# Strassen's seven block products for gate and value of two sequences, with TensorE in the order of the program text

## Chip, cores, metric

One core of one Trainium2 chip. The metric is the device time of one execution in microseconds (us), as the median of several runs. All timed runs quoted here were in the fast state; single looks (one run, state unknown) are marked as such.

## The reference

Attention with normalised q and k over 8 sequences of 448 tokens and 12 heads of 64, followed by a gated feed-forward layer. All in float32 on the chip; the weights arrive in 8-byte form and are converted on the chip.

```python
batch, n_heads, seq, head_dim = (8, 12, 448, 64)       # attention
n_tokens, d_model, d_ff = (3584, 768, 1536)            # feed-forward

scores = scale * np.matmul(rmsnorm(q, g_q), rmsnorm(k, g_k).transpose(0, 1, 3, 2))
attn = softmax(scores)                                 # cut: max, exp, sum
x = np.matmul(attn, v)                                 # (B,H,S,D) -> (B*S, H*D)
xn = x / rms(x) * rms_g
g = xn @ w_gate
return (g * (1 / (1 + np.exp(-g))) * (xn @ w_val)) @ w_out
```

## The kernel before

A program text that mixes two streams: attention of sequence b, pair of heads by pair, and feed-forward items of sequence b-1, put into four slots of each pair by `fill()`. The scheduler of the framework then orders each engine by priority and simulated readiness. The parts that matter:

```python
ps_s, ps_m, ps_f = pool("c_ps_s", 4, space=PSUM), pool("c_ps_m", 2, space=PSUM), pool("c_ps_f", 2, space=PSUM)
...
def turn(g, i):                     # transpose q or k of a pair
    ps = ps_m.tile([128, NT, P], F32, name="tr", tag="m")
    ...                             # four transposes; i == 0: ScalarE copies, i == 1: VectorE copies
def values(g):
    av = st["av", g] = ps_m.tile([128, 512], F32, name="av", tag="m")
    ...                             # e @ v, then den = sums of e (four terms in the first sequence, else one)
def divide(g):
    nc.vector.reciprocal(rd, den[:, 0:S])
    nc.vector.tensor_tensor(x, av[:, 0:S], rd, ALU.mult)
    ...                             # x*x on ScalarE, ss += on GpSimd
def project(b, fc, w):              # one of 12 column blocks of gate or value
    ps = st[w, b, fc] = ps_f.tile([128, 512], F32, name="ff", tag="ff")[:, 0:S]
    for c in range(NDC):            # 6 matmuls
        nc.tensor.matmul(ps, lhsT=wt[:, c, :], rhs=st["xT", b][:, c, :], start=(c == 0), stop=(c == NDC - 1))
...
for g in range(NG):                 # 48 pairs
    score(g, (0, 1)); norm_pair(g + 2); fill()
    turn(g + 1, 0); fill()
    if g: finish(g - 1)             # values, divide, fill
    turn(g + 1, 1); score(g, (2, 3)); fill()
```

`convert` turns a weight block to float32: a DMA, then ScalarE, GpSimd, VectorE twice, ScalarE, GpSimd. In the kernel before a third of the blocks is converted beside sequence 0's attention, the rest beside its feed-forward.

## Time and profile before

| | kernel before |
|---|---|
| time | 1848.26 us median (1848.02 to 1853.11, 4 runs) |
| TensorE busy | 1778.2 us, 96% |
| to the first gate matmul | 138 us, sequence 0 alone |
| 138 to 300 us | units beside conversion, 21 us of TensorE idle |
| 300 us to the end | TensorE never idle until its last matmul, 432.9 us for two sequences, 216.4 for one |

How to read it: "busy" on TensorE hides gaps shorter than a matmul's modelled end, so I go by spacings, start to start. Most lines are in the prediction. The first gate matmuls of sequences 2, 4 and 6 start at 602.45, 1035.33 and 1468.20 us. Windows, columns: length; TensorE, weight load, VectorE, ScalarE and GpSimd, each as busy us and records; clock, DMA share, GB/s.

### The profile page before, as it was taken

To read this page: it belongs to the slowest core of one execution; us is meant where nothing else is said; L and a number is where in the kernel's file an instruction comes from. 1 tells how busy PE (TensorE), PEld (TensorE's weight loads), DVE (VectorE), ACT (ScalarE), POOL (GpSimd) and SP (SyncE) were. 2 spreads that over 40 slices of the span, in tenths; PEclk is the share of its full clock that TensorE was granted. 3 is DMA by queue.
4 is the path that set the end of the run, shared out by engine and by line. 5 is a ranking of instruction groups with operands and counts; after the bars stand their busy time and mean duration, and the time that the engine had idled before them with its cause. 6 is when DMAs were issued, how large, how long until landed. Compare 5 with 4: busy or idle time off the path is not lost. (4 is left out here: it accounts for less than half of the span.)

```text
span 1848.4 us, 15816 instructions
## 1 busy us (share of the span) xinstructions
PE 1778.2 (96%) x5960; PEld 880.4 (48%) x5960; DVE 510.6 (28%) x546; ACT 441.8 (24%) x725; POOL 638.1 (35%) x527
## 2 busy tenths in 40 slices
PE   5878989999999999999999999999999999999998
PEld 2333434544455444554455544554445544455554
DVE  3646664122212222123212222222221222111100
ACT  5643442122121313112221122212222122210000
POOL 6765774324232424322432243323234133210000
PEclk9888999999999999999999999999999999999999
DMA  5625653122220323113321232212231132202200
GB/s 157 219 76 156 194 190 99 32 82 80 87 55 27 90 83 93 46 53 88 87 65 38 66 91 83 68 41 84 84 90 41 41 87 67 69 18 74 88 9 28
DMA packets 154475, 149.00 MB, mean 81 GB/s; under 512 B 95509, under 2 KB 124693, under 8 KB 154389
## 3 DMA queue, kind: packets, MB, share of 16 engines
q1 hardware_dynamic: 153280, 147.88, 27.6%
q8 instruction: 50, 0.82, 0.2%
q14 instruction: 37, 0.29, 0.1%
q10 hardware_dynamic: 1108, 0.00, 0.0%
HBM read 127.41 MB, written 20.45 MB: 80 GB/s over the span
## 5 line engine op out<-in xcount | busy, mean ns | idle before, releaser
L578 PE MATMUL ff<-xT,wg 128*128 128x448 f32 x1152 | 457.0, 547 | 7.3 <-DVE ga L587 7.2
L578 PE MATMUL ff<-xT,wv 128*128 128x448 f32 x1152 | 456.6, 546 | 3.4 <-DVE hT L593 3.4
L603 PE MATMUL ff<-wo,hT 128*128 128x384 f32 x1344 | 444.6, 488 | 0.0
L603 PEld LDWEIGHTS ff<-wo,hT 128*128 128x128 f32 x1344 | 251.6, 190 | 182.2 <-issue 14.9
L578 PEld LDWEIGHTS ff<-xT,wg 128*128 128x128 f32 x1152 | 215.7, 191 | 231.6 <-issue 212.0
L578 PEld LDWEIGHTS ff<-xT,wv 128*128 128x128 f32 x1152 | 214.3, 191 | 229.6 <-issue 215.3
L511 POOL TENSOR_TENSOR es<-es,e 112x448 f32<-112x448 f32 x168 | 187.0, 1145 | 289.3 <-ACT e L501 289.3
L501 ACT ACTIVATE e<-sc,rs 112x448 f32<-112x448 f32 x384 | 214.2, 636 | 160.8 <-PE sc L497 160.7
L497 PE MATMUL sc<-qkT 64*112 64x448 f32 x768 | 185.4, 590 | 21.8 <-DVE qkT L487 15.2
L546 POOL TENSOR_TENSOR ss<-ss,s 128x448 f32<-128x448 f32 x40 | 46.6, 1164 | 427.4 <-ACT s L545 427.4
L535 DVE RECIPROCAL rd<-den 128x448 f32<-128x448 f32 x48 | 141.9, 2956 | 180.6 <-PE den L526 180.6
L519 PE MATMUL av<-e,vt 112*64 112x448 f32 x768 | 159.1, 557 | 0.0
L466 POOL TENSOR_TENSOR rs<-ms,mhalf 112x16 f32<-112x16 f32 x48 | 140.4, 2926 | 4.0
L585 ACT ACTIVATE th<-ff 128x448 f32<-128x448 f32 x96 | 52.0, 541 | 342.5 <-PE ff L578 342.4
L587 DVE SCALAR_TENSOR_TENSOR ga<-th,ff 128x448 f32<-128x448 f32 x96 | 59.2, 617 | 252.8 <-ACT th L585 252.8
L593 DVE SCALAR_TENSOR_TENSOR hT<-ga,ff 128x448 f32<-128x448 f32 x96 | 59.3, 618 | 236.5 <-PE ff L578 232.6
L463 DVE TENSOR_REDUCE ms<-sq 112x16 f32<-112x1024 f32 x48 | 58.5, 1219 | 216.8 <-ACT sq L460 201.2
L497 PEld LDWEIGHTS sc<-qkT 64*112 64x112 f32 x768 | 66.7, 180 | 104.4 <-issue 58.0
L507 POOL TENSOR_TENSOR es<-e 112x448 f32<-112x448 f32 x84 | 94.1, 1140 | 50.7 <-ACT e L501 50.7
L545 ACT ACTIVATE s<-xT 128x448 f32<-128x448 f32 x40 | 23.1, 577 | 327.7 <-DVE xT L540 327.7
L519 PEld LDWEIGHTS av<-e,vt 112*64 112x64 f32 x768 | 52.0, 140 | 97.7 <-issue 97.4
L468 POOL TENSOR_TENSOR qn<-qk,rs 112x512 f32<-112x512 f32 x48 | 51.4, 1070 | 80.8 <-PE tr L482 79.8
(46 smaller groups left out, 709.9 us busy)
## 6 DMA issues: line engine op xcount, KB each, us to landing
wg<-kept_g SPq DMA_DIRECT2D x84, 384.0 KB, 3.0
wv<-kept_v SPq DMA_DIRECT2D x84, 384.0 KB, 3.0
qk<-in_q_dram SPq DMA_DIRECT2D x96, 112.0 KB, 3.3
qk<-in_k_dram SPq DMA_DIRECT2D x96, 112.0 KB, 3.2
vt<-in_v_dram SPq DMA_DIRECT2D x48, 224.0 KB, 2.6
raw<-in_moe_w_gate_dram SPq DMA_DIRECT2D x12, 768.0 KB, 5.9
raw<-in_moe_w_val_dram SPq DMA_DIRECT2D x12, 768.0 KB, 4.8
raw<-in_moe_w_out_dram SPq DMA_DIRECT2D x12, 768.0 KB, 4.5
```

The source lines that it names most:

```text
L463: nc.vector.tensor_reduce(out=ms, in_=sq.rearrange("p (n d) -> p n d", d=D), axis=AX_X, op=ALU.add)
L466: nc.gpsimd.tensor_tensor(rs, ms, mhalf[0:P, :], ALU.pow)
L497: nc.tensor.matmul(ps, lhsT=qkT[r, 1, c * P:(c + 1) * P], rhs=qkT[r, 0, :], start=True, stop=True)
L501: nc.scalar.activation(e, ps, ACT.Exp, scale=rs[:, n:n + 1])
L507: nc.gpsimd.tensor_tensor(es, st["e", g, 0, j], st["e", g, 1, j], ALU.add)
L511: nc.gpsimd.tensor_tensor(es, es, st["e", g, c, j], ALU.add)
L519: nc.tensor.matmul(av[j * D:(j + 1) * D, 0:S], lhsT=vt[:, j, c, :], rhs=st["e", g, c, j], start=(c == 0), stop=(c == NT - 1))
L535: nc.vector.reciprocal(rd, den[:, 0:S])
L578: nc.tensor.matmul(ps, lhsT=wt[:, c, :], rhs=st["xT", b][:, c, :], start=(c == 0), stop=(c == NDC - 1))
L587: nc.vector.scalar_tensor_tensor(ga, th, 1.0, g, ALU.add, ALU.mult)
L593: nc.vector.scalar_tensor_tensor(hT[:, fc, c0:c0 + S], st.pop(("ga", b, fc)), 0.5, st.pop(("v", b, fc)), ALU.mult, ALU.mult)
L603: nc.tensor.matmul(ps, lhsT=hT[:, fc, i * 128:(i + 1) * 128], rhs=wo[:, fc, n * HALF:(n + 1) * HALF], start=(fc == 0), stop=(fc == NFC - 1))
```

## The change

Intent: with two sequences stacked, gate (and value) is a 2x2 block product: rows are two sequences, the inner dimension is cut in half, and column block fp is paired with fp+6. Strassen's form (Winograd's variant) needs seven products of half the size instead of eight, so 1/8 of the matmuls of gate and value go. To keep the order in which products follow each other, TensorE is taken from the scheduler and runs in the order of the text. What it takes: feed-forward can start only after two sequences, the weights are stored as seven combined blocks and loaded from DRAM for each two sequences, and the eight PSUM banks are split 4, 1 and 3 instead of 4, 2 and 2. Conversion now goes by half blocks, with two buffers for raw words instead of three.

```diff
-    ps_s, ps_m, ps_f = pool("c_ps_s", 4, ...), pool("c_ps_m", 2, ...), pool("c_ps_f", 2, ...)
+    ps_s, ps_m, ps_f = pool("c_ps_s", 4, ...), pool("c_ps_m", 1, ...), pool("c_ps_f", 3, ...)
+    ORDER = ("B11", "T2", "B21", "T3", "T4", "T1", "B22")
@@ turn
-        ps = ps_m.tile([128, NT, P], F32, name="tr", tag="m")
+        ps = (ps_f if i == 1 and g <= ALONE else ps_m).tile(...)        # ALONE: sequences 0 and 1
@@ in place of project, gate, val
+    def product(k, fp, w, left, right, bank, onto=False):              # 3 matmuls; onto: adds to the bank
+        def p1(): product(.., "A11", "B11", fresh("a")); nc.scalar.copy(add["p1"], bank["a"])
+        def p6(): product(.., "S2", "T2", fresh("b")); plus("u2", bank["b"], "p1")
+        def p2(): product(.., "A12", "B21", bank["a"], onto=True); hand(0, 0, bank["a"])
+        def p7(): product(.., "S3", "T3", fresh("c")); plus("u3", bank["c"], "u2")
+        def p4(): product(.., "A22", "T4", fresh("d")); plus("c21", bank["d"], "u3"); hand(1, 0, add["c21"])
+        def p5(): product(.., "S1", "T1", fresh("e")); plus("c22", bank["e"], "u3")
+        def p3(): product(.., "S4", "B22", bank["e"], onto=True); plus("c12", bank["e"], "u2"); hand(0, 1, ..); hand(1, 1, ..)
+        return [p1, p6, p2, p7, p4, p5, p3]
@@ ffn_items: 84 products spread over 24 slots of the next sequence, 14 output items over those of the one after
+    AHEAD, LEFT = 14, 3
@@ before the main loop
+    ctx.enter_context(tc.manual_schedule(engines={mybir.EngineType.PE}))
@@ weights: conversion of units 0 and 1 in sequence 1; the rest, and the output weight, in sequence 2
```

(cut: loading, left factors, the rest of `ffn_items`)

## The prediction

> **What bounds the kernel now.** I read the page first (shares, forty slices), then the busy time by windows, then the time line of single stretches. The page says that TensorE is the bound, and the slices say where it is not.
>
> ```profile
> PE 1778.2 (96%) x5960; PEld 880.4 (48%) x5960; DVE 510.6 (28%) x546; ACT 441.8 (24%) x725; POOL 638.1 (35%) x527
> PE   5878989999999999999999999999999999999998
> PEclk9888999999999999999999999999999999999999
> ...
> L578 PE MATMUL ff<-xT,wg 128*128 128x448 f32 x1152 | 457.0, 547 | 7.3 <-DVE ga L587 7.2
> L578 PE MATMUL ff<-xT,wv 128*128 128x448 f32 x1152 | 456.6, 546 | 3.4 <-DVE hT L593 3.4
> ```
>
> The second view is the busy time by windows:
>
> ```profile
> 138.00:300.00 162.00, 141.27 (x432) 64.70 (x432) 101.70 (x88) 67.36 (x98) 111.03 (x82) 0.92 0.55 171
> 300.00:1627.00 1327.00, 1327.00 (x4511) 659.81 (x4511) 316.85 (x354) 289.21 (x498) 429.39 (x366) 1.00 0.24 68
> ```
>
> So three stages. To 138 us (the first gate matmul) one sequence's attention runs alone. From 138 to 300 gate and value of sequence 0 run while weights are still converted: 21 us of TensorE idle, clock 0.92. From 300 on TensorE never rests: 1327/6 = 221.2 us a sequence, at full clock. The change takes TensorE work away, and it pays only where TensorE stays this full. Whether it does is the question.
>
> The third view is the time line of TensorE and VectorE:
>
> ```profile
> 1675.86 4.67 PE L578 MATMUL ff<-xT,wv 128*128 128x448 f32 x12
> 1680.37 4.67 PE L578 MATMUL ff<-xT,wg 128*128 128x448 f32 x12
> ```
>
> Start to start is 4.51 us for 12 records. A float32 matmul is two records (1152 records, 576 matmuls), so one is 0.752 us and one product of three matmuls 2.26 us. In the same way an output item of 24 records is 7.79 us, a score call 1.69, av 3.06, den from summed e 0.85, four transposes 0.45: a pair is 2x1.69+2x0.45+3.06+0.85 = 8.2, a sequence with its norm 50.8. The steady stage then is 24x4.51+7x7.79+50.8 = 213.5 us by spacings against 221.2 measured: 7.7 us a sequence go at switches between kinds.
>
> **What the Trainium skill says.** "TensorE: Matmul & The Clock Gate", Part 1, says that the array falls to half clock after an idle window of about 3.4 us. The trace agrees: the first line below needs 6.47 us for what takes 4.7, so such a gap costs 1.8 us more.
>
> ```profile
> 202.19 6.47 PE L578 MATMUL ff<-xT,wg 128*128 128x448 f32 x12 [3.75 <-DVE ga L587]
> ```
>
> The same page, Part 2, says that matmuls stay in program order and only weight loads are pulled ahead; and, under "Architectural detail", that ScalarE and VectorE are strict first in, first out. So a matmul whose bank is not free holds all behind it; the line above is such a wait. "PSUM — Partial Sum Buffer", on the has_written bits, says that a matmul without the first flag adds to what is there; the change uses this to save two additions per unit. It is not exercised like that before, so no trace shows it yet. "Advanced Engine Details and Errata", "VectorE Performance Modes", says that VectorE's second SBUF port is shared with GpSimd and they block each other. The conversion's shift agrees: 0.55 us alone, 2.19 beside a GpSimd addition of 1.85.
>
> **The change, part by part.** Two sequences are one 2x2 block product; "unit" is my word for seven products of gate or value (12 units for two sequences).
>
> Removed: 48 items of 4.51 us become 84 products of 2.26, so 216.5 -> 189.4 us per two sequences, **27.1 us saved, 108 us in all**. Output work is the same (14 items for two sequences, 109 us).
>
> Added on VectorE: five additions and four hand-overs of 0.62 us a unit, 5.6 us beside 15.8 us of matmuls. Not a bound by itself. But three things now wait in TensorE's fixed order.
> (a) Products p5 and p3 stand next to each other, and p3 adds onto p5's bank after VectorE has read it (c22). The loss is 0.16 drain + 0.1 start + 0.62 + 0.05 (VectorE's ga ended at 165.33, the matmul started at 165.38) = 0.95 us a unit, 48 units: 46 us. No slot falls between the two: the fill rule gives 3, 4, 3, 4 products, so it breaks after p2 and after p3. p2 onto p1's bank has p6 between, no wait.
> (b) The pool of transposes and av has one bank instead of two. In program order the second transpose of the next pair follows av and den, and needs av's bank. The chain behind den, and the one that the row norm needs, stand here:
>
> ```profile
> 1008.28 2.96 DVE L535 RECIPROCAL rd<-den 128x448 f32<-128x448 f32 x1 [11.53 <-PE den L526]
> 1011.27 0.62 DVE L540 TENSOR_TENSOR xT<-av,rd 128x448 f32<-128x448 f32 x1
> 1011.99 0.58 ACT L545 ACTIVATE s<-xT 128x448 f32<-128x448 f32 x1 [7.13 <-DVE xT L540]
> 1012.64 1.13 POOL L546 TENSOR_TENSOR ss<-ss,s 128x448 f32<-128x448 f32 x1 [14.98 <-ACT s L545]
> ```
>
> The bank comes free 3.7 us after den's end, ss 5.6 us after. In the sequences that fill with products every slot has 7 or 9 us of work and covers this. In those that fill with output items, 11 items go to 24 slots: by the rule to slots 2,4,6,8,10,13,15,17,19,21,23. The slot after av and den is each fourth one, so it is filled at 4 and 8 and empty at 12, 16, 20 and 24. Three empty ones cost 3.7+1.8 (cold clock) = 5.5 each, the last one waits for ss, 5.6+1.8 = 7.4; three empty slots between the first transpose and av cost some 1.0 each, two between the score calls 1.0 each. **29 us in each of three such sequences, 87 us.**
> (c) Sequences 0 and 1 run without filler. A pair there has four den terms, 3.0 instead of 0.85: 10.4 us of work, plus 2.1 waiting for av's bank behind four exponentials, plus 2.3 because the copy of the second transpose queues behind the reciprocal, plus 2 for the clock: 17 us (18.0 in the kernel before, 63.75 to 81.73, with two conversions a pair).
>
> Stages, in us:
> 1. To the first product: 16 start, 6 for the first pair, 11x17, then scores, av, den, ss chain, norm and score calls of the next, 26: **235**.
> 2. Sequence 2 with 84 products and conversions: 189.4+50.8+7.7+12x0.95 = 259. Here fall 64 half blocks of conversion. VectorE: 64x1.3 (94.5 us for 36 full blocks) = 83, 40 subtractions estimated at 0.5 = 20, units 67, attention 33, norm 4: 207 of 259, 80%, against 63% in the window 138 to 300, where 24 full blocks cost 34 us of idle and slow clock. I choose 41 us of loss: **300**.
> 3. Sequences 3, 5, 7 with output items: 109+50.8+4+29 = 193 each, **579**.
> 4. Sequences 4, 6 with products: 259 each, **518**.
> 5. The tail: 189.4+11.4+109+7 (the end after the last matmul, as now) = **317**.
> Sum **1949**. Against 1848: -108 saved, +13 for den terms, and the rest is waiting.
>
> **Rivals.** (R1) The saving survives: the waits of (a) and (b) are covered because other engines run ahead, and conversions hide. The 2-unit lead of the conversions and the 14 blocks of weights asked ahead speak for it; that the order is the text's speaks against. Stages 210+265+3x165+2x248+306 = 1772 us. (R2) Conversion becomes the bound of stage 2: two raw buffers instead of three, each held from the DMA (4.5 to 5.9 us to landing for a full block) through six operations. In the window 138 to 300 a full block took 6.75 us with three buffers. If a half block takes 6 us with two, 64 take 384 us and the total is some 2030. Against it: half sizes and more lead. (R3) Weights from DRAM hold TensorE: a block of 192 KB per 2.26 us is 87 GB/s, and 231 GB/s have been moved in the trace, while 384 KB landed in 3.0 us. With 14 blocks ahead I expect nothing of it. (R4) Only one of (a) and (b) is real: about 1865 to 1905.
>
> **Range and chances.** I lean from the sum a little towards R1, since waits estimated one by one overlap: 1935 us, 8 in 10 between 1835 and 2030. The lower end is half of (a) and (b) with a stage 2 without loss; the upper is R2. Faster by over 2% (under 1811) needs R1 nearly whole: 0.12. Within 2%: 0.20. Slower: 0.68.
>
> **What would show it.** In the changed profile: 2016 gate and value matmul records for 1152x2 = 2304 times 7/8 (right by counting); the first product near 235 us; idle of TensorE before p3 by VectorE's c22, 48 times near 0.8 us; idle before the second transpose by VectorE's x, some 3.5 us, three times in each of sequences 3, 5 and 7, with a clock under 1.0 there; slices of 7 to 8 tenths in these stretches and 9 in sequences 4 and 6. I am wrong if TensorE stays full from 300 us on, if the bank waits are absent, or if the first stages take under 470 us (R1) or over 600 us (R2) in sum.

## More of the kernel before

```profile
602.40:1035.30 432.90, 432.90 (x1474) 215.48 (x1472) 104.55 (x117) 95.31 (x165) 143.27 (x121) 1.00 0.25 70
1035.30:1468.20 432.90, 432.90 (x1475) 215.50 (x1473) 104.56 (x117) 95.42 (x165) 143.24 (x121) 1.00 0.25 70
```

Two sequences are compared with 432.9 us below.

## The result

The changed kernel took **2000.6 us** (1998.36 to 2005.86, 4 runs), the kernel before 1848.26. The ratio is 1.082, 95% interval 1.079 to 1.085. Here and below a ratio is the mean of one kernel's fast runs over the mean of the other's of the same rounds, so it is not quite the ratio of the medians. The time lies inside the range, towards its upper end; slower was the direction with chance 0.68.

The page of the changed kernel (busy time, slices of 50 us, granted clock):

```profile
PE 1749.4 (87%) x5744; PEld 854.5 (43%) x5744; DVE 713.7 (36%) x966; ACT 482.1 (24%) x897; POOL 615.7 (31%) x559
...
PE   5767687778689988999999988999999998999998
...
PEclk8788888899889988999999988999999998999999
...
L624 PE MATMUL ff<-x,wt 128*128 128x448 f32 x2016 | 807.5, 554 | 107.2 <-DVE c L638 98.3
```

2016 gate and value records, 7/8 of 2304: the work did go away. TensorE is less busy and the span is longer, so waiting more than took its place. The busy time by windows, cut at the stage borders (columns as above):

```profile
0.00:254.30 254.30, 173.66 (x736) 72.36 (x736) 101.44 (x127) 100.87 (x189) 103.75 (x95) 0.85 0.30 80
254.30:596.50 342.20, 262.32 (x767) 120.97 (x765) 196.13 (x296) 114.79 (x223) 171.02 (x177) 0.90 0.46 141
596.50:795.20 198.70, 177.23 (x638) 93.11 (x637) 50.92 (x57) 44.62 (x82) 72.63 (x61) 0.93 0.21 58
795.20:1047.30 252.10, 243.49 (x766) 113.35 (x764) 99.38 (x138) 58.86 (x108) 70.47 (x59) 1.00 0.30 83
```

Sequences 3 and 4 together take 450.8 us, against 432.9 for two sequences before: even in the steady part the saved 27 us are lost, and 18 more. Who TensorE waited for (sum in us, times, longest):

```profile
PE ff L624 <- DVE c L638: 98.3, 48, 10.8
PE av L548 <- ACT qkT L514: 36.1, 21, 5.5
PE tr L511 <- issue: 30.3, 8, 3.8
PE sc L526 <- DVE qkT L516: 29.7, 15, 4.9
PE msx L588 <- POOL ss L576: 28.2, 5, 5.7
```

Each line is one of the waits of the prediction (`tr` are transposes, `sc` scores, `msx` the sums of the row norm, which needs all squares `ss`). The first is p3's wait for c22, 48 times (the profile leaves numbers out of names, so c21, c22 and c12 all stand as c, and u2 and u3 as u). The third says "issue", that is, no releaser found; the time line of sequence 3 shows what it is:

```profile
705.32 2.96 DVE L564 RECIPROCAL rd<-den 128x448 f32<-128x448 f32 x1 [18.48 <-PE den L555]
708.31 0.62 DVE L571 TENSOR_TENSOR x<-av,rd 128x448 f32<-128x448 f32 x1
...
709.03 0.98 PE L511 MATMUL tr<-ident,qk 112*128 112x112 f32 x4 [3.79 <-issue]
709.94 3.33 PE L526 MATMUL sc<-qkT 64*112 64x448 f32 x8
```

VectorE ends x at 708.93 and the transposes start at 709.03: they waited for av's bank. What follows runs cold: 0.98 and 3.33 us for what takes 0.55 and 1.76 when TensorE is warm.

### The profile page after: what moved, and what is told of

The parts are those of the page before. It is cut to its first block, busy times and chain, and to the rows that moved or that the text cites. A ratio compares the mean times of both kernels' runs of the same rounds, so it can differ in the third digit from the quotient of the medians.

```text
span 2004.0 us, 16820 instructions
## 1 busy us (share of the span) xinstructions
PE 1749.4 (87%) x5744; PEld 854.5 (43%) x5744; DVE 713.7 (36%) x966; ACT 482.1 (24%) x897; POOL 615.7 (31%) x559
## 4 chain that ended last, share of the span: by engine, by line
PE 66%; DVE 3%; issue 2%; DMA 1%; POOL 1%; ACT 1%; SPq 0%; ACTq 0%; POOLq 0%; DVEq 0%
PE ff L624 30%; PE ff L691 23%; PE sc L526 6%; PE av L548 5%; PE tr L511 1%; DVE c L638 1%; PE den L555 1%; DMA raw<-in_moe_w_out_dram 1%; DVE x L602 1%; DVE rd L564 0%; PE msx L588 0%; DMA qk<-in_k_dram 0%; ACT qkT L514 0%; PE rb L598 0%; SPq L478 0%
## 5 line engine op out<-in xcount | busy, mean ns | idle before, releaser
L624 PE MATMUL ff<-x,wt 128*128 128x448 f32 x2016 | 807.5, 554 | 107.2 <-DVE c L638 98.3
L624 PEld LDWEIGHTS ff<-x,wt 128*128 128x128 f32 x2016 | 378.9, 193 | 520.1 <-issue 365.3
L691 PE MATMUL ff<-wt,hT 128*128 128x384 f32 x1344 | 457.8, 500 | 0.0
L691 PEld LDWEIGHTS ff<-wt,hT 128*128 128x128 f32 x1344 | 259.5, 196 | 196.9 <-issue 33.0
L530 ACT ACTIVATE e<-sc,rs 112x448 f32<-112x448 f32 x384 | 216.4, 633 | 233.4 <-PE sc L526 231.1
L576 POOL TENSOR_TENSOR ss<-ss,rd 128x448 f32<-128x448 f32 x40 | 46.6, 1166 | 380.2 <-ACT rd L575 360.9
L638 DVE TENSOR_TENSOR c<-ff,u 128x448 f32<-128x448 f32 x144 | 89.8, 623 | 167.4 <-PE ff L624 167.1
L491 DVE TENSOR_REDUCE ms<-sq 112x8 f32<-112x512 f32 x96 | 65.7, 684 | 140.0 <-ACT sq L490 139.9
L427 POOL TENSOR_TENSOR wt<-top,raw 128x384 int32<-128x384 int32 x72 | 76.3, 1063 | 68.6 <-DVE top L424 29.0
L575 ACT ACTIVATE rd<-x 128x448 f32<-128x448 f32 x40 | 23.0, 574 | 275.1 <-DVE x L571 275.1
L423 DVE TENSOR_SCALAR top<-top 128x384 int32<-128x384 int32 x72 | 36.2, 503 | 137.7 <-POOL top L421 137.7
```

The costliest lines, as they stand in the source:

```text
L427: nc.gpsimd.tensor_tensor(dst.rearrange("p a n -> p (a n)").bitcast(I32), top, lo, ALU.add)
L491: nc.vector.tensor_reduce(out=ms[:, i * n // 2:(i + 1) * n // 2], in_=sq.rearrange("p (n d) -> p n d", d=D), axis=AX_X, op=ALU.add)
L530: nc.scalar.activation(e, ps, ACT.Exp, scale=rs[:, n:n + 1])
L624: nc.tensor.matmul(bank[:, 0:S], lhsT=wt[:, c * 128:(c + 1) * 128], rhs=x[:, c, :], start=not onto and c == 0, stop=c == 2, skip_group_che ...
L638: nc.vector.tensor_tensor(add[name], ps[:, 0:S], add[other], ALU.add)
L691: nc.tensor.matmul(ps, lhsT=h[:, i * 128:(i + 1) * 128], rhs=st["wo", k, n, fc], start=(fc == 0), stop=(fc == NFC - 1))
```

## The experiments

Theory: the loss is a sum of separate waits that the text's order exposes. (a) p3 directly after p5, whose bank it adds to. (b) One bank for transposes and av. (c) Output items that leave the slot behind av and den empty. (d) Conversion beside the units, with VectorE's queue standing. Rivals: VectorE is behind in general and waits only move; the fixed order costs by itself; the seven products cannot be fed at all.

All ratios are against the kernel before, run in the same rounds on the same chip. "Stages" are: to the first product; from there to the first output item; sequences 3 and 4.

| run | time, us | ratio | first product | first output | seq. 3 | seq. 4 |
|---|---|---|---|---|---|---|
| changed kernel | 2000.6 | 1.082 | 254.4 | +342.1 | 198.8 | 252.1 |
| e1_swap | 1961.0 | 1.060 | 257.6 | +327.9 | 198.8 | 240.8 |
| e2_turn_f | 1923.9 | 1.041 | 223.4 | +349.7 | 176.4 | 252.8 |
| e3_left2 | 1953.8 | 1.057 | 254.4 | +341.8 | 175.3 | 255.8 |
| e4_out_early | 1993.6 | 1.078 | 275.0 | +313.1 | 200.5 | 252.7 |
| e5_sched | 1893.4 | 1.023 | 226.3 | +334.3 | 181.5 | 243.3 |
| e7_no_dve (wrong) | 1973.9, one run | - | 255.5 | +310.0 | 199.8 | 251.9 |
| e9_all | 1863.4 | 1.007 | 259.3 | +294.3 | 172.1 | 246.7 |
| e10_all_sched | 1840.7 | 0.995 | 253.7 | +294.8 | 169.3 | 241.8 |
| e14_light_conv (wrong) | 1738.3, one run | - | 204.0 | +239.6 | 169.3 | 242.3 |

The stages are read from the starts of TensorE's records in each profiled run.

### e1_swap: p4 between p5 and p3

```diff
-    ORDER = ("B11", "T2", "B21", "T3", "T4", "T1", "B22")
+    ORDER = ("B11", "T2", "B21", "T3", "T1", "T4", "B22")
-        return [p1, p6, p2, p7, p4, p5, p3]
+        return [p1, p6, p2, p7, p5, p4, p3]
```

> p5 and p4 change places (and their weight blocks in the stored order), so that p4's matmuls lie between p5 and p3, which adds onto p5's bank. Theory (the adjacency costs about 0.9 us a unit, and more in sequence 2 where VectorE is late): the 0.72 us waits before p3 go in sequences 4, 6 and the tail (36 units, 33 us), in sequence 2 the waits before p3 (72.5 us in the changed kernel) shrink by some 2.3 us a unit at most; time 1945 to 1965. Rival (VectorE is behind in general, the wait only moves to another matmul): waits of the same sum elsewhere, 1985 or more.

Measured: 1960.98 us (1956.79 to 1963.73), ratio 1.060 (1.058 to 1.062). The wait in the changed kernel, and the same four products (p7 to p3) with the swap:

```profile
832.32 0.62 DVE L638 TENSOR_TENSOR c<-ff,u 128x448 f32<-128x448 f32 x1 [0.97 <-PE ff L624]
...
833.00 2.52 PE L624 MATMUL ff<-x,wt 128*128 128x448 f32 x6 [0.72 <-DVE c L638]
```

```profile
813.30 9.29 PE L624 MATMUL ff<-x,wt 128*128 128x448 f32 x24
```

Six records stand apart in the first, all 24 run in one piece in the second. Sequence 4 falls by 11.3 us, 0.94 us a unit. Sequence 2 gains 14 us only: its waits before p3 fall from 72.5 to 40.7 us, but 13.5 us more than before come up in front of other products. So the rival holds in part, and in sequence 2 alone.

### e2_turn_f: both transposes from the pool of three

```diff
-        ps = (ps_f if i == 1 and g <= ALONE else ps_m).tile([128, 512], F32, name="tr", tag="f" if ... else "m")
+        ps = ps_f.tile([128, 512], F32, name="tr", tag="f")
```

> Both transposes of a pair take their bank from the pool of three (as the second one does already in sequences 0 and 1), so that the one-bank pool holds av alone. Theory (the single bank makes the waits): the 3.79 us waits before the second transpose in sequences 3, 5, 7 go (9 of them, with the cold clock after them about 50 us) and the waits of av on the copy of the first transpose go (36 us, 30 of them in the stage before the first product, with their clock up to 45); time 1905 to 1925. Rival (the reciprocal chain on VectorE is the real chain, the bank only shows it): the score call of the next pair waits for the copy behind the reciprocal instead, gain half, 1945 to 1970.

Measured: 1923.94 us (1922.91 to 1928.71), ratio 1.041 (1.039 to 1.043). An empty slot in sequence 3 of this run:

```profile
648.94 0.92 PE L555 MATMUL den<-es,ones 112*64 112x448 f32 x4
649.79 0.60 PE L511 MATMUL tr<-ident,qk 112*128 112x112 f32 x4
650.33 1.76 PE L526 MATMUL sc<-qkT 64*112 64x448 f32 x8
```

The transposes follow den at once and stay warm. Score calls wait for the copy of a transpose for 2.3 us in this whole sequence, so the rival's wait did not come. 31 us came from the start (both norms and 12 pairs), 22.4 from sequence 3. Of the single edits that keep the text's order this one gains most, and no memory was needed for it, only another pool.

### e3_left2: one output item in each even slot

```diff
-    AHEAD, LEFT = 14, 3
+    AHEAD, LEFT = 14, 2
```

> LEFT 3 to 2: 12 instead of 11 output items are spread over the 24 slots, which by the fill rule puts one in each even slot, so that the slot after av and den is always filled, the last one too, and one item fewer is kept for the end. Theory (empty slots expose the bank wait and the wait for ss): waits before the second transpose (11.4 us a sequence) and before the row sums (5.6) in sequences 3, 5, 7 go with about 6 us of cold clock, some 5 us come back where the normalisation and the left factors have less to hide behind; about 18 us a sequence, time 1940 to 1955. Rival (the waits are not from the slots): no change within 5 us.

Measured: 1953.82 us (1950.60 to 1957.03), ratio 1.057 (1.055 to 1.059). Sequence 3 falls by 23.5 us, as much as by e2: both remove the same wait, one by a bank and one by work in front of it. So the two gains don't add: with both (e9, below) the sequence takes 172.1 us, 3 to 4 us less than with one. The next sequence gets back 3.7 us, where some 5 were expected for one item less at its start. It is the same constant that pads the last slot, so that the row norm's wait (5.6 us in the changed kernel's sequence 3) is gone too.

### e5_sched: the seven products, the scheduler's order

```diff
-    ctx.enter_context(tc.manual_schedule(engines={mybir.EngineType.PE}))
```

> The changed kernel without the fixed order of TensorE: the scheduler orders it, as in the kernel before. This separates the two halves of the change. If the order of the text is what exposes the waits, this is faster than 2000 us: 1900 to 1960, with TensorE filled in sequences 3, 5 and 7. If the units themselves are what cannot be kept fed (three banks, one shared bank, conversions), it is 2000 or slower, with waits in other places.

Measured: 1893.35 us (1890.67 to 1894.09), ratio 1.023 (1.021 to 1.025). This is under the expected 1900 to 1960. So of the 152 us lost, 107 go with the fixed order, and 45 stay without it. Windows of sequences 3 and 4 in this run:

```profile
560.60:742.00 181.40, 173.52 (x644) 91.02 (x644) 51.75 (x60) 47.31 (x85) 79.74 (x67) 0.98 0.24 64
742.00:985.30 243.30, 243.30 (x759) 114.30 (x758) 98.11 (x134) 57.85 (x103) 62.97 (x53) 1.00 0.31 86
```

TensorE has no idle in sequence 4 and 8 us in sequence 3, against 8.6 and 21.5 us. The scheduler puts other matmuls in between: from 861.91 us, for example, a product runs between two parts of a score call.

### e6_before_text: the kernel before, order of the text

```diff
+    ctx.enter_context(tc.manual_schedule(engines={mybir.EngineType.PE}))
     for g in range(3):
         load_pair(g)
```

> The kernel before with TensorE's order fixed to the text, nothing else. The changed kernel loses 107 us by the fixed order (2000.6 against 1893.4 without it). If the fixed order is costly in itself, this loses about as much: 1930 or more. If it is costly only together with the single shared bank, the adjacent products and the empty slots, this stays near: its slots take at least one gate or value item of 4.5 us each, which covers the 3.7 us of the reciprocal chain, and only the output part has an empty slot in six: 1850 to 1890.

Measured: 1847.41 us (1846.80 to 1848.53), ratio 0.9989 (0.9972 to 1.0005), the same time, and less than the 1850 to 1890 that I expected. In the kernel before, the fixed order costs nothing by itself. My reading is that it costs where a matmul's bank is not free when its turn comes, and that the kernel before, with at least two banks in each pool, hardly has such places.

### e4_out_early and e7_no_dve: conversion beside the units

e4 moves the 24 half blocks of the output weight from sequence 2 to sequence 0:

```diff
-        if 5 <= u - 2 < 2 * NFP - 1:                        # in make(u)
-            for fc in range(2 * (u - 7), 2 * (u - 6)):
-                make_out(fc)
+        if b == 0:                                           # in the main loop
+            make_out(2 * hp)
+            make_out(2 * hp + 1)
```

> The 24 half blocks of the output weight are converted during sequence 0, four a pair, instead of during sequence 2. Theory (sequence 2 waits because VectorE's queue stands behind conversions, 72.5 us before p3 in the changed kernel): 24 of 64 half blocks leave it, the stage from first product to first output item falls from 342 to 305 to 320 us, and the stage before the first product grows by 5 to 15 us, as GpSimd and VectorE have room there (104 and 101 us busy of 254). Time 1970 to 1990. Rival (the gate and value units' own conversions and subtractions make the wait): stage 330 or more, time 1995 or more.

Measured: 1993.60 us (1992.86 to 1997.87), ratio 1.078 (1.077 to 1.080). The time is above the expected 1970 to 1990. Sequence 2 gives 29.0 us, the start takes 20.6: conversion costs nearly as much beside attention alone as beside the units. That the start had room, judged by busy times, was wrong.

e7 leaves out the two VectorE instructions of `convert`; its result is wrong.

```diff
-        nc.vector.tensor_scalar(top, top, 3, 0x3FFFFFF8, ALU.logical_shift_left, ALU.bitwise_and)
-        nc.vector.scalar_tensor_tensor(top, hi, -(2**30), top, ALU.bitwise_and, ALU.bitwise_or)
```

> Wrong result on purpose: the changed kernel with the two VectorE instructions of the conversion left out (shift and sign), all else as it is. Theory (VectorE's first-in first-out queue stands at the shift, which waits for GpSimd's clamp, while u3, c21 and c22 are queued behind): the waits before p3 in sequence 2 fall from 72.5 to under 35 us, the stage from 342 to 285 to 310 us; the subtractions of blocks still wait there. Rival (the blocks themselves come late through DMA and GpSimd): the waits stay within 20% or turn into waits of the products for their blocks.

Measured: 1973.88 us in one run. Sequence 2 falls from 342 to 310 us. Its waits (same view as above, 250 to 600 us):

```profile
PE ff L621 <- ACT p L652: 24.0, 6, 8.0
PE ff L621 <- DVE c L635: 20.4, 12, 4.0
```

The wait for c22 fell from 72.5 to 20.4 us, but 24.0 us came up as a wait of p2 for ScalarE's copy of p1 (2.1 us before). The first reading held: VectorE's queue stood at the shift. The rival as I put it did not show, since no product waited for its block. But once VectorE's queue doesn't stand, ScalarE's shows: in sequence 2 of this run ScalarE is idle for 124.9 us with the first operation of a conversion next in its queue, until the raw words have come. This is how VectorE's queue stands, in the changed kernel at its first unit:

```profile
270.89 0.52 POOL L421 TENSOR_SCALAR top<-top 128x384 f32<-128x384 f32 x1
...
271.44 1.30 DVE L423 TENSOR_SCALAR top<-top 128x384 int32<-128x384 int32 x1 [5.10 <-POOL top L421]
272.78 0.74 DVE L424 SCALAR_TENSOR_TENSOR top<-raw,top 128x384 int32<-128x384 int32 x1
...
273.65 1.01 POOL L427 TENSOR_TENSOR wt<-top,raw 128x384 int32<-128x384 int32 x1 [0.55 <-issue]
273.71 0.61 DVE L638 TENSOR_TENSOR u<-ff,u 128x448 f32<-128x448 f32 x1
...
274.69 0.38 SPq L415 DMA_DIRECT2D raw<-in_moe_w_gate_dram  x1
275.00 0.61 DVE L638 TENSOR_TENSOR c<-ff,u 128x448 f32<-128x448 f32 x1
...
277.95 0.54 ACT L420 ACTIVATE top<-raw 128x384 f32<-128x384 f32 x1 [1.67 <-DMA raw<-in_moe_w_gate_dram]
...
279.12 0.36 DVE L423 TENSOR_SCALAR top<-top 128x384 int32<-128x384 int32 x1 [2.18 <-POOL top L421]
279.40 0.62 DVE L638 TENSOR_TENSOR c<-ff,u 128x448 f32<-128x448 f32 x1
...
280.07 4.80 PE L624 MATMUL ff<-x,wt 128*128 128x448 f32 x6 [7.59 <-DVE c L638]
```

VectorE sits idle for 5.1 us with the shift at the head of its queue, until GpSimd has clamped; u3 and c21, whose products are long done, stand behind it; c22 comes last, and p3 waits 7.6 us, then runs at half speed (4.80 instead of 2.52).

The shift in front of c22 (279.12) shows one thing more. Its raw words are asked for at 274.69, when GpSimd's last addition for an earlier block ends (274.66) and one of the two raw buffers comes free, and ScalarE can start on them at 277.95. So the transfer is part of the chain. In sequence 2 of the changed kernel ScalarE stood idle so for 141 us:

```profile
ACT top L420 <- DMA raw<-in_moe_w_out_dram: 55.1, 22, 6.3
ACT top L420 <- DMA raw<-in_moe_w_val_dram: 44.8, 15, 5.5
ACT top L420 <- DMA raw<-in_moe_w_gate_dram: 40.8, 14, 6.2
```

A third raw buffer, which might let a transfer start earlier, was not run.

### e9_all, e12_spread: all four remedies, order of the text

e9 has the edits of e1, e2, e3 and e4 together. e12 differs in that the output weight's conversions are spread over sequences 0 and 1 (`if b < 2: make_out(g)`).

> All four remedies together, order of the text kept: p5 before p4, both transposes from the pool of three, LEFT 2, output weights converted during sequence 0. If the causes are separate, stages add up: about 232 to the first product, 310 to the first output item, then 174, 241, 174, 244, 168 and 302 for the tail: 1845, within 20 us. If they overlap, 1870 to 1890. Sequences 3 to 7 should then show the units' saving: about 415 us for two sequences against 442 in the kernel before.

> All four remedies, text order, but the output weight's 24 half blocks converted two a pair over sequences 0 and 1 instead of four a pair in sequence 0. In the run before, waits of the score calls up to 10 us stood in sequence 0 (128 us to its norm, against 105 for sequence 1). If those come from four conversions a pair being more than the gaps of a pair hold, the first product comes at 240 to 250 us instead of 259 and the time is 1845 to 1855; if any conversion there costs about the same, it stays at 1860 or more.

Measured: e9 1863.40 us (1861.77 to 1863.75), ratio 1.007 (1.005 to 1.009); e12 1861.11 us (1857.15 to 1864.02), ratio 1.006 (1.005 to 1.008). e9 is 18 us over the sum of parts that I had put together, inside "within 20". It is also 33 us over what the four single gains would give if they added, since e2 and e3 remove the same waits. Sequences 3 and 4 now take 418.8 us, 14 less than two sequences before (the 442 of the expectation is the misread figure). The start does not move with the place of the conversions: 256.4 us to the first product in e12, 259.3 in e9, so the second reading of e12 holds: the row norm of sequence 0 comes 8.7 us earlier in e12, and sequence 1 takes 5.8 us longer.

### e10_all_sched, e13_spread_sched: the remedies with the scheduler's order

> The kernel of the run with all four remedies (1863.4 us), but with TensorE's order left to the scheduler. On the changed kernel the fixed order cost 107 us. If the four remedies took away what the fixed order exposed, the scheduler has little left to fill: 1845 to 1870, and both orders are within 1%. If the fixed order hides yet another cost, this is under 1830.

> The spread conversions with the scheduler's order: the best of what the runs point to. 1835 to 1850 if both gains add, and so at most 1% faster than the kernel before; the start (attention of two sequences alone, then units beside conversion, some 540 us for what the kernel before has done in about 500) is what is left of the loss.

Measured: e10 1840.65 us (1836.90 to 1843.41), ratio 0.9952 (0.9939 to 0.9966); e13 1840.98 us (1840.69 to 1843.55), ratio 0.9961 (0.9948 to 0.9975). Both are faster than the kernel before by 0.4 to 0.5%: the intervals exclude 1. e10 is under the expected 1845 to 1870, and the scheduler's order is still worth 23 us, 1.2%, where I had expected 1% at most. Windows of the first two stages of e10, and of sequence 3:

```profile
0.00:253.70 253.70, 174.76 (x747) 71.38 (x748) 124.24 (x170) 124.48 (x239) 146.79 (x146) 0.84 0.48 135
253.70:548.50 294.80, 254.94 (x756) 118.23 (x755) 174.61 (x253) 89.36 (x172) 125.11 (x125) 0.93 0.38 116
548.50:717.70 169.20, 168.38 (x637) 90.03 (x637) 43.04 (x50) 44.23 (x82) 72.63 (x61) 1.00 0.25 70
```

Two sequences take 411.1 us against 432.9: 22 of the 27 us are saved here, and 42 us for sequences 3 to 6. In the profiled runs the kernel ends only 7 us ahead, so the rest of it has cost some 35 us more than before.

### e14_light_conv: what the start waits for

The kernel of e10 with a conversion of a DMA and one ScalarE copy; wrong, one run.

```diff
-        ...                                    # six operations
+        nc.scalar.activation(dst.rearrange("p a n -> p (a n)"), hi.bitcast(F32), ACT.Copy)
```

> Wrong result on purpose: the kernel with the four remedies and the scheduler's order, in which a conversion is its DMA and one ScalarE copy of half of the words instead of six operations. It splits the start of 548 us (to the first output item) into conversion and the rest. If conversion beside attention and beside the units holds TensorE, the start falls to 470 to 500 us (about 225 to the first product, then 250 to 270) and the time to 1765 to 1795; if the start is long because two sequences' attention runs without filler and the queues of VectorE are behind anyway, it stays above 525 us and the time above 1815.

Measured: 1738.32 us, under the range that I expected. The first two stages:

```profile
0.00:204.00 204.00, 164.21 (x746) 68.61 (x747) 80.12 (x94) 107.28 (x199) 85.87 (x72) 0.94 0.59 168
204.00:443.60 239.60, 239.58 (x756) 114.07 (x755) 132.02 (x185) 76.98 (x140) 69.17 (x55) 1.00 0.49 143
```

The start falls from 548 to 444 us, 50 and 55 us by stage, and TensorE is full in sequence 2. The transfers are as many and as large, so their load alone does not hold TensorE; what was removed is the chain of operations on three engines. With it, however, a raw buffer comes free after one operation instead of six, so the next transfer starts sooner: up to the first output item ScalarE waits 37 us for raw words here, against 182 in e10. The operations and the wait for one of two raw buffers are not told apart by this run. This doesn't say that the units would win by 110 us with a lighter conversion: the kernel before would gain too, and that was not run.

## Why the prediction was right, and where its sizes were off

| stage | predicted | measured |
|---|---|---|
| 1. to the first product | 235 | 254 |
| 2. sequence 2 with conversions | 300 | 342 |
| 3. sequences 3, 5, 7 with output items | 579 | 586 |
| 4. sequences 4, 6 with products | 518 | 506 |
| 5. tail | 317 | 316 |
| sum | 1949 | 2004 |

(The measured column is the profiled run.)

**The base: misread.** 1327 us hold more than six sequences (see the profile before), so a sequence took 216.4 us, not 221.2, and the switches between kinds cost 2.9 us, not 7.7. Stage 4 carries the 7.7 twice: that is 10 of the 12 us by which it came out too long. It offset a part of what stages 1 and 2 lacked, by luck.

**(a) p3 behind p5: right.** 0.95 us a unit predicted; 0.72 us of idle seen, 0.94 us a unit gained in sequence 4 by e1, 0.98 in the tail (315.8 to 304.1 us).

**(b) The single bank and the empty slots: right, with the slots named.** 3.7 us predicted, 3.79 seen; three such waits in sequence 3 (8 in all, 9 expected); ss 5.6 predicted, 5.62 seen. e2 and e3 each removed them. 29 us a sequence predicted; 23.5 us went with e3 alone. The cold clock was undersized: after the wait for ss the next output item (773.66) took 10.94 us, the one after it (785.32) 7.92: 3.0 us, where I had put 1.8.

**(c) Sequences 0 and 1 alone: right in kind, 19 us short.** The term that failed is the 26 us "then scores, av, den, ss chain, norm": I counted that norm chain once, for sequence 1. Sequence 0 has it as well, and nothing lies beside it: den ended at 132.0 us and the next transposes began at 142.5. Also the pairs of sequence 0 took 15 to 22 us, not 17.

**Stage 2: right in kind, the size failed.** I chose 41 us of loss by VectorE's busy share (80% against 63%); it was 83 by the prediction's own sum. e7 and e14 show why a share was the wrong measure: VectorE is not full (196 of 342 us), it stands idle at the head of its queue waiting for GpSimd, and the additions that free p3's bank stand behind. In the kernel before an item of 4.5 us lies between a bank and its next use; here p3 needs the answer at once. e1 gave it one more product of time and sequence 2 gained 14 us.

**The lean towards R1 was wrong.** I took 14 us off the sum because waits estimated one by one might overlap. The sum was under the measured time, not over it. (The gains of the remedies do overlap, as e9 shows; that says nothing for the lean.) Without the lean and with the second norm chain the prediction had been some 1960.

**R2 (conversion as the bound)** came half true: the stage took 342, not 384 us, and the first two stages 596.5 us, just under the 600 that I had named as its sign. The wait of the conversions for one of two raw buffers, on which it rests, is in the trace (e7, above). The measured time lies inside the range because R2 had set the upper end; the sum alone was some 52 us short. **R3 (weights from DRAM)** was rightly set aside: no wait of a product for a block's DMA stands among TensorE's waits. **R4** is what e2 and e1 look like alone, at 1924 and 1961 us, higher than I had put it, since the first two stages were longer.

What stays open: why a conversion costs the start as much with two a pair as with four (e12, e13); what a third raw buffer would give; and whether the kernel before with a light conversion would keep ahead of e14.

## What to carry to other kernels

A saving in TensorE's work is worth what the rest lets it be: before taking matmuls away, list for each matmul of the new order whose bank it needs and which engine frees it, and put another product between the two. A fixed order was free in the kernel before (e6) and costly where banks were not free in time (e5), so fix the banks and the slots first, then compare orders. Judge an in-order engine by what stands at the head of its queue, not by its busy share.

## What the Trainium skill lacked or had wrong

- "TensorE: Matmul & The Clock Gate", "Why this matters for your kernels", advises to have no idle gap over some 3 us. In sequence 1 of the changed kernel no listed gap within the pairs is so long: gaps of about 1.5 and 2.6 us in each pair of 16 us went with a granted clock of 0.91 (147 to 238 us), and av took 4.92 us instead of 3.23 in most pairs. Before av, however, only four transposes of 0.60 us lie between the gap and the scores. From the scores' end to av it is 2.95 to 3.19 us (pairs from 164 us on), so that a limit under 3 us is not shown.
- "PSUM — Partial Sum Buffer", on the has_written bits, tells that a matmul can add to a bank, but not what it costs to add onto a bank that another engine reads in between: 0.72 us of idle and 0.94 us of time each, with a 0.62 us addition on VectorE (e1).
- "Trainium Kernel Development and Optimization", "Best Practices", calls occupancy fine as a measure of the distance to roofline for the engines other than TensorE. It does not show what an engine makes others wait: in sequence 2 VectorE was busy 57% (196.13 of 342.20 us), and TensorE waited 72.5 us for its additions. The wait at the head of its queue (5.10 us at 271.44) shows it.
- No page has the cost of this conversion chain beside matmuls: 105 us of start for 72 half blocks with two raw buffers (e10 against e14, one run).
